# Four rows of the first pair read from stacked q and k, and the low-rank weights converted over more slots

## The chip, the cores and the metric

The kernel runs on one core of a Trainium2 chip. The metric is the device time of one execution in microseconds (us), as the median of three runs. The profile is one further execution, recorded by the hardware profiler. Engines are named as the trace names them: PE is TensorE's matmul, PEld its weight load, DVE is VectorE, ACT is ScalarE, POOL is GpSimd, and SP is SyncE, which only issues transfers. A trailing q (SPq, ACTq) is an engine's instruction queue.

## What is computed

An attention with a threshold feeds two token-mixing blocks. The part that the change touches is the attention and the low-rank mix behind it; the dense products behind them are named because their weights are converted meanwhile.

```python
scores = scale * (q @ k.T)                      # 4 batches, 8 heads, 576 rows, 64 wide
thresh = max(scores, axis=-1) - tau
attn = exp(where(scores >= thresh, scores, -1e9) - max)
attn = attn / (sum(attn) + 1e-9)
x = (attn @ v)                                  # heads side by side: 512 wide
u = x + (x.T @ U @ V).T                         # U: 576 x 32, V: 32 x 576
y = u + relu(u @ w_ch1) @ w_ch2                 # 512 x 2048 and 2048 x 512
out = (sigmoid(causal_conv(y, conv_w)) * (y @ w_val)) @ w_out
```

The weights U, V, w_ch1, w_ch2, w_val, conv_w and w_out come in as 64-bit floats and are converted on the chip.

## The kernel before

**Pairs and slots.** Two heads make a pair; there are 16 pairs. A pair has nine row blocks of 128: row 0 holds the last 64 rows of both heads, rows 1, 3, 5, 7 are 128-row blocks of the first head, rows 2, 4, 6, 8 of the second. The loop over `s` walks 144 slots, one row block in each: slot `s` is row `s % 9` of pair `s // 9`. Every engine gets its instructions in the order in which the loop writes them, so the order is set by hand. In slot `s`, VectorE scales the scores of its row and takes the maximum (`soft_max`, L467), masks the exponentials of the row before (`soft_mask`, L492) and, in the first pair only, adds the threshold (L482; in the others GpSimd does it). ScalarE takes the exponential (L481) and copies transposed blocks out of PSUM (L517 and others). TensorE computes the scores of the next row (`next_scores`), and transposes the exponentials of the row two slots back (L508, L525). The scores have two PSUM tiles, so row s+1 can be computed once L467 of slot s-1 is done. The product with v (`pv`, L551 and L562) for rows 0 to 4 of a pair comes in its last slot, for rows 5 to 8 four slots later; then the result is transposed back (`back`) and divided by the sums into `ring`.

**Precision.** q and k are split into a high and a low part (`hi_lo_qk`, L356 and L359, for a later pair's transposed q and k). A score is hi x hi + hi x lo + lo x hi + lo x lo. For pairs from the second on, `stacks` copies the parts by SyncE's transfers into a tile `st` for each head: its first 64 partitions hold high q, the other 64 low q; below stand high k twice and low k twice. With 128 partitions in use, two matmuls for each half of 288 columns do a row. The first pair doesn't wait for such transfers: `st` of the first pair has q's high and low parts in that head's 64 partitions and zeros in the others (L639), and a row takes four matmuls for each half (first head, L453), or four for each of three pieces (second head, L446, since its columns stand in another order). The tiles `st` come from a pool of four.

**Weights.** A converter is a generator of steps (`from_f64`: L101 on ScalarE, L103, L106, L110, L114, L122 or L124, L129 on VectorE or GpSimd). `work.tick()` moves each of at most two live converters on by one step. `wtick` says in which slots a tick comes: in each of the first 18 slots and in slots 3, 4 and 8 once more, then in six of every 18 (`CONVERT_AT`). U and V (`setup_UV`, in two parts, 512 and 224 wide) begin in slot 4, the four row blocks of the first quarter of w_ch1 (`chunk(0, 0)`, loads on L160) in slot 6, w_ch2's in slot 110.

**The mix.** `mix_t` (L601, x by U), `mix_tt` (a transpose), `mix_ut` and `mix_u` (by V, adding x) of pair p come 16, 18, 20 and 20 slots after its first. The first pair's are the first to need U and V.

Of the kernel before, what the change touches and what calls it, by code (L numbers as in the profile page):

```python
# [22 lines left out]
F32R = mybir.dt.float32r  # L23
# [13 lines left out]
def attention_moe_kernel(  # L37
# [15 lines left out]
    nc = tc.nc  # L53
    B, H, S, D = q.shape
# [11 lines left out]
    SM = 512  # L66
    TL = S - SM
# [9 lines left out]
    def f(ap):  # L77
        return ap.bitcast(F32)
# [165 lines left out]
    CONVERT_AT = (0, 2, 9, 12, 13, 17)  # L244
# [14 lines left out]
    def attention(dense_front, dense_mid, dense_top, dense_left, dense_back):  # L259
# [9 lines left out]
        st_p = front.enter_context(tc.tile_pool(name="st", bufs=4, side="right"))  # L269
# [16 lines left out]
        st8 = [dict() for _ in range(NP)]  # L286
# [114 lines left out]
        def stacks(p, hh):  # L401
# [13 lines left out]
            nc.sync.dma_start(out=s[64:128, 0, :], in_=qk[a:a + 64, 3, :])  # L415
            st8[p]["st", hh] = st

        def tails(p):
            qk = st8[p]["qk"]
            t = bd[p % 2]  # L420
            for hh in range(2):
                a = hh * D
                for c, sl in ((0, 0), (1, 3)):
                    o, i = t[a:a + 64, c, a:a + 64], f(qk[a:a + 64, sl, SM:S])
                    nc.gpsimd.tensor_scalar(out=o, in0=i, scalar1=1.0, scalar2=0.0, op0=ALU.mult, op1=ALU.add)


        def scores(p, i):
            d = st8[p]
            s = s_ps.tile([128, 2, 512], F32, tag="s", name="s")  # L430
            if i == 0:
                qk, t = d["qk"], bd[p % 2]
                ops = [(t[:, 0, :], qk[:, 1, :]), (t[:, 1, :], qk[:, 1, :]), (t[:, 0, :], qk[:, 2, :])]
            else:
                c, hh = divmod(i - 1, 2)
                c *= 128
                if p:
                    st = d["st", hh]
                    lhs = st[:, 0, c:c + 128]
                    ops = [(lhs, st[:, 1, :]), (lhs, st[:, 2, :])]  # L440
                else:
                    ops = [(d["st", hh][:, m, c:c + 128], d["qk"][:, n, :]) for m in (0, 1) for n in (1, 2)]
                    if hh:
                        for o, n, a in ((s[:, 0], TL, SM), (s[:, 0, TL:], HS - TL, 0), (s[:, 1], HS, HS - TL)):
                            for m, (lhs, rhs) in enumerate(ops):
                                nc.tensor.matmul(  # L446
                                    o[:, 0:n], lhs, rhs[:, a:a + n], start=(m == 0), stop=(m == len(ops) - 1)
                                )
                        d["s", i] = s
                        return  # L450
            for n in range(2):
                for m, (lhs, rhs) in enumerate(ops):
                    nc.tensor.matmul(  # L453
                        s[:, n, 0:HS], lhs, rhs[:, n * HS:(n + 1) * HS], start=(m == 0), stop=(m == len(ops) - 1)
                    )
            d["s", i] = s
# [32 lines left out]
        def soft_mask(p, i):  # L489
            d = st8[p]  # L490
            e = row(p, i)
            nc.vector.scalar_tensor_tensor(  # L492
                out=e, in0=d.pop(("ns", i)), scalar=d.pop(("th", i))[:, 0:1], in1=e, op0=ALU.is_le, op1=ALU.mult,
                accum_out=d["sum"][:, i:i + 1],
            )
            if i == 8:
                t = d["sum"]
                nc.vector.tensor_scalar(out=t, in0=t, scalar1=1e-9, scalar2=None, op0=ALU.add)
                nc.vector.reciprocal(out=d["r"], in_=t)
# [137 lines left out]
        for hh in range(2):  # L637
            t = st8[0]["st", hh] = st_p.tile([128, 3, S], F32R, tag="st", name="st")
# [4 lines left out]
        for m in range(2):  # L643
# [7 lines left out]
            out=rv[0][:, 0:8 * R].rearrange("p (t r) -> p t r", t=4),  # L651
            in_=moe_U[0:SM, :].rearrange("(t p) r -> p t r", p=128),
# [3 lines left out]
        def load_V(a, o, c, n):  # L656
            for g in range(4):
                nc.gpsimd.dma_start(out=a[g * R:(g + 1) * R, o:o + n], in_=moe_V[:, c:c + n])
# [3 lines left out]
            out=qscale, in0=tau_sb, scalar1=0.0, scalar2=-(float(D) ** -0.5), op0=ALU.is_ge, op1=ALU.mult  # L662
# [13 lines left out]
        for m in range(4):  # L676
            for _, fn in late[m].pop(-2, []):
                fn()
        load_V(rv[1], 0, 2 * (FC - nu), 2 * (nu + S - FC))


        def setup_UV(part):
# [17 lines left out]
        def put(s, what, *a):  # L700
            slots[s].append((what, a))

        for p in range(NP):
            s0 = 9 * p
            end = p == NP - 1
            for i in range(9):
                put(s0 + i + 2, trans_main, p, i)
                if i % 2 == 0:
                    put(s0 + i + 2, trans_tail, p, i)
            put(s0 + 8, pv, p, *(0, 1))  # L710
            v2 = s0 + (13 if end else 12)
            put(v2, pv, p, *(2,))
            put(v2 + 1, back, p)
            if p + 1 < NP:
                for what, at, *a in ((prep_T, (-3, 0), "q"), (prep_T, (1, 1), "k"), (prep_T, (2, 2), "tail"),
                    (stacks, (3, 5), 0), (tails, (4, 5)), (stacks, (5, 3), 1)):
                    put(s0 + at[not p], what, p + 1, *a)
            put(s0 + (15 if end else 16), mix_t, p)
            put(s0 + (17 if end else 18), mix_tt, p)
            put(s0 + (18 if end else 20), mix_ut, p)  # L720
            put(s0 + (18 if end else 20), mix_u, p)
        def next_scores(s):
            scores(*divmod(s + 1, 9))

# [2 lines left out]
        for s in range(NS):  # L727
            p, i = divmod(s, 9)
            slot[0] = s
            live = p < NP  # L730
            ev = slots[s]
            if s == 4:
                work.add(setup_UV(0))
                work.add(setup_UV(1))
            if s == 6: chunk(0, 0)
            if s == 110: chunk(0, 1)
            work.width = 2 if s < 9 * NP - 9 else 4
            def wtick(at):
                if at == 0 and (s < 18 or s % 18 in CONVERT_AT) or at == 1 and s in (3, 4, 8):
                    work.tick()  # L740
            wtick(-1)
            if live:
                soft_max(p, i)
            for m in (0, 1, 2, 3):
                for _, fn in sorted(late[m].pop(s, []), key=lambda x: x[0]):
                    fn()
                if m == 1 and live:
                    soft_exp(p, i)
                if m == 0 and 1 <= s <= 9 * NP:
                    soft_mask(*divmod(s - 1, 9))  # L750
                wtick(m)
            wtick(4)
            if s + 1 < 9 * NP:
                ev = [(next_scores, ())] + ev
            for what, a in sorted(ev, key=lambda x: 9 if x[0] in last else ORDER.get(x[0].__name__, 5)):
                what(*a) if what in last else what(s, *a)
            if i == 0 and p + 2 < NP:
                loads.append(load_qk(p + 2))
            if i == 4 and p + 1 < NP:
                loads.append(load_v(p + 1))  # L760
            load(2)
            if s == 9 * NP - 1:
                front.close()
                steps = next(dense_front)
                later(s + 1, 3, lambda: list(steps))
            if s == 9 * NP:
                ps_s.close()
            if s == 9 * NP + 1:
                mid.close()
                dense_mid()  # L770
            if s == 9 * NP + 5:
                top.close()
                dense_top()
                work.finish()
                chunk(1, 0)
            if s >= 9 * NP:
                next(dense_front, None)
                for _ in range(1 if lots else 1):
                    work.tick()
# [16 lines left out]
    def chunk(c, part):  # L796
        if c < NCH:
            src = w_ch2[c * FC:(c + 1) * FC, :] if part else w_ch1[:, 2 * c * FC:2 * (c + 1) * FC]
        else:
            src = w_out if part else w_val  # L800
        if 1 <= c < NCH and not part:
            loaded_rows = []
            for kk in range(KD):
                work.add(stage_rows(loaded_rows, kk, src[kk * 128:(kk + 1) * 128, :], c))
            work.add(combine(rows.setdefault((c, part), []), loaded_rows, c))
            return
        for kk in range(KD):
            work.add(weight_rows(rows.setdefault((c, part), []), (w2 if part else w1)[c % 2], kk, src[kk * 128:(kk + 1) * 128, :],
              (nc.vector if part else nc.vector) if c == 0 else nc.gpsimd,
              *(((0, 0, nc.gpsimd) if part else (0, 0, nc.gpsimd)) if c == 0 else ())))  # L810
# [490 lines left out]
```

## Time and profile before

| | |
|---|---|
| median of three runs | 802.89 us (802.13, 802.89, 803.55) |
| the profiled execution's own time | 802.15 us |
| its span, first to last instruction | 800.1 us |
| PE busy | 794.1 us (99%) |
| DVE busy | 684.2 us (86%) |
| ACT busy | 438.9 us (55%) |
| POOL busy | 196.9 us (25%) |
| granted TensorE clock over the span | 1.00 |

The attention's slots run from 9.56 us (first L467) to about 306 us; the rest of the span is dense products. Busy shares are averages over stages. A matmul's end is modelled, and neighbours overlap, so the interval between starts tells more than a duration does. A row of the chain says what held up the last instruction at that time, a row of the timeline what an engine did.

### The profile page before, as it was taken

How to read it: one execution, taken by the hardware profiler on the slowest of the kernel's cores; microseconds unless marked ns; L12 is line 12 of the kernel's file. 1: busy time of each engine (PE TensorE's matmuls, PEld its weight loads, DVE VectorE, ACT ScalarE, POOL GpSimd, SP SyncE). 2: the span in 40 equal slices, each digit the busy share in tenths (PEclk: the TensorE clock that was granted, in tenths of full speed). 3: DMA queues.
4: the chain of work that ended last, by engine and by line, in shares of the span. 5: the costliest groups of instructions: out<-in, count | busy, mean ns of one | idle time of the engine just before them, and what ended most of it. 6: DMA issues, size and time to landing. Idle time of an engine off the chain costs nothing.

```text
span 800.1 us, 15270 instructions
## 1 busy us (share of the span) xinstructions
PE 794.1 (99%) x5292; PEld 721.4 (90%) x5292; DVE 684.2 (86%) x1484; ACT 438.9 (55%) x943; POOL 196.9 (25%) x280
## 2 busy tenths in 40 slices
PE   9999999999999999999999999999999999999998
PEld 8788888888888888788899999999999999988887
DVE  7999999988888999579979799689999998988740
ACT  6888988888888888453423225123343343355421
POOL 4633533433333342030141004200342110000000
PEclk9999999999999999999999999999999999999999
DMA  7766776666667453556768658377477573001112
GB/s 166 185 149 149 171 171 152 145 142 137 149 160 167 105 132 134 168 181 252 279 224 309 219 198 302 111 271 288 165 274 261 188 246 119 1 1 52 54 53 79
DMA packets 97685, 134.20 MB, mean 168 GB/s; under 512 B 51285, under 2 KB 62309, under 8 KB 97610
## 3 DMA queue, kind: packets, MB, share of 16 engines
q1 hardware_dynamic: 96074, 132.24, 54.6%
q8 instruction: 42, 0.69, 0.3%
q0 software_dynamic: 336, 0.74, 0.3%
q10 hardware_dynamic: 1200, 0.26, 0.2%
q14 instruction: 33, 0.27, 0.1%
HBM read 85.43 MB, written 21.23 MB: 133 GB/s over the span
## 4 chain that ended last, share of the span: by engine, by line
PE 95%; DVE 3%; issue 1%; DMA 0%; SPq 0%; DVEq 0%
PE s L453 10%; PE c L1197 9%; PE a L1197 9%; PE a L1159 8%; PE c L1159 8%; PE xm L508 7%; PE o L562 7%; PE a L903 6%; PE v L903 6%; PE c L903 6%; PE p L1099 6%; PE xs L601 2%; PE o L551 2%; PE tm L380 2%; PE xs L562 1%; PE xs L525 1%
## 5 line engine op out<-in xcount | busy, mean ns | idle before, releaser
L467 DVE TENSOR_SCALAR_CACHE_REDUCE ns<-s,scalars 128x576 f32<-128x576 f32 x144 | 116.6, 810 | 18.1 <-PE s L453 17.5
L482 POOL TENSOR_TENSOR th<-nm,scalars 128x1 f32<-128x1 f32 x135 | 86.7, 642 | 161.1 <-DVE ns L467 158.2
L492 DVE SCALAR_TENSOR_TENSOR e<-ns,th,e 128x576 f32<-128x576 f32 x144 | 118.9, 826 | 0.0
L481 ACT ACTIVATE e<-ns,nm 128x576 f32<-128x576 f32 x144 | 112.2, 779 | 8.2 <-DVE ns L467 6.6
L453 PE MATMUL s<-st 128*128 128x288 f32 x480 | 94.2, 318 | 0.1
L517 ACT ACTIVATE pt<-xm 128x512 f32<-128x512 f32 x144 | 85.9, 597 | 4.5 <-PE xm L508 3.0
L508 PE MATMUL xm<-idn,e 128*128 128x128 f32 x576 | 86.8, 273 | 0.0
L1197 PE MATMUL a<-region,w 128*128 128x384 f32 x432 | 81.1, 335 | 0.2 <-DVE region L1130 0.2
L1197 PE MATMUL c<-region,w 128*128 128x384 f32 x432 | 80.7, 334 | 0.0
L453 PEld LDWEIGHTS s<-st 128*128 128x128 f32 x480 | 68.6, 191 | 12.3 <-issue 7.3
L1136 ACT ACTIVATE region<-c_sb 128x384 fp32r<-128x384 f32 x72 | 37.5, 524 | 73.4 <-DVE c_sb L1135 73.4
L1197 PEld LDWEIGHTS a<-region,w 128*128 128x128 f32 x432 | 75.3, 188 | 0.7 <-DVE region L1130 0.7
L1159 PE MATMUL a<-region,w_s 128*128 128x384 f32 x378 | 75.8, 334 | 0.0
L1159 PE MATMUL c<-region,w_s 128*128 128x384 f32 x378 | 75.6, 334 | 0.0
L1197 PEld LDWEIGHTS c<-region,w 128*128 128x128 f32 x432 | 75.5, 188 | 0.0
L508 PEld LDWEIGHTS xm<-idn,e 128*128 128x128 f32 x576 | 69.7, 143 | 0.7 <-issue 0.2
L174 POOL TENSOR_TENSOR w<-wf,w 128x512 fp32r<-128x512 f32 x20 | 29.0, 1451 | 162.3 <-ACT w L172 154.3
L1159 PEld LDWEIGHTS c<-region,w_s 128*128 128x128 f32 x378 | 66.4, 188 | 0.0
L1159 PEld LDWEIGHTS a<-region,w_s 128*128 128x128 f32 x378 | 66.3, 188 | 0.1
L562 PE MATMUL o<-pt,vt 128*64 128x256 f32 x512 | 61.5, 382 | 0.0
L562 PEld LDWEIGHTS o<-pt,vt 128*64 128x64 f32 x512 | 34.0, 137 | 19.2 <-issue 5.3
L1099 PE MATMUL p<-w,region 128*128 128x512 f32 (+1 forms) x228 | 49.8, 378 | 0.0
(166 smaller groups left out, 1514.6 us busy)
## 6 DMA issues: line engine op xcount, KB each, us to landing
region<-sp SPq DMA_DIRECT2D x126, 384.0 KB, 5.3
raw<-in_moe_w_ch_dram SPq DMA_DIRECT2D x32, 512.0 KB, 4.6
sp<-c_sb SPq DMA_DIRECT2D x24, 384.0 KB, 2.4
st<-qk SPq DMA_DIRECT2D x30, 256.0 KB, 3.4
st<-qk SPq DMA_DIRECT2D x45, 144.0 KB, 3.4
st<-qk SPq DMA_DIRECT2D x15, 432.0 KB, 4.0
out_dram<-c_sb SPq DMA_DIRECT2D x17, 256.0 KB, 2.0
st<-qk SPq DMA_DIRECT2D x15, 288.0 KB, 4.8
```

Of the source, the lines that this page charges most:

```text
L453: nc.tensor.matmul(s[:, n, 0:HS], lhs, rhs[:, n * HS:(n + 1) * HS], start=(m == 0), stop=(m == len(ops) - 1))
L467: nc.vector.tensor_scalar(out=ns.rearrange("p (a b) -> p a b", a=2), in0=s, scalar1=qscale[:, 0:1], scalar2=3.0e38, op0=ALU.mult, op1=ALU. ...
L481: nc.scalar.activation(out=row(p, i), in_=d["ns", i], func=ACTF.Exp, bias=nm[:, 0:1], scale=-1.0)
L482: (nc.gpsimd if p or 0 else nc.vector).tensor_tensor(out=th, in0=nm, in1=tau_eff, op=ALU.add)
L492: nc.vector.scalar_tensor_tensor(out=e, in0=d.pop(("ns", i)), scalar=d.pop(("th", i))[:, 0:1], in1=e, op0=ALU.is_le, op1=ALU.mult, accum_o ...
L508: nc.tensor.transpose(x[:, j * 128:(j + 1) * 128], e[:, c + j * 128:c + (j + 1) * 128], idn)
L517: later(s + 1, 0, lambda: nc.scalar.activation(out=dst, in_=x.rearrange("p (j c) -> p j c", j=4), func=ACTF.Copy), "x")
L562: nc.tensor.matmul(o, lhs, rhs, start=False, stop=stop)
L903: nc.tensor.matmul(ps[:, 0:m1], lhs, rhs, start=(m == 0), stop=(m == len(ops) - 1))
L1099: nc.tensor.matmul(ps, t[:, a, kk, sl], w[:, bb, kk, cols], start=(m == 0), stop=(m == 3 * KD - 1))
L1159: nc.tensor.matmul(ps, lhs, rhs, start=k == 0, stop=k == 5)
L1197: nc.tensor.matmul(ps, lhs, rhs, start=k == 0, stop=k == 3 * KD - 1)
```

## The change

Three things change. Rows 5 to 8 of the first pair are read from stacked tiles as those of the later pairs are: `first_stacks` makes them by four transfers on ScalarE's queue (first head) and six on SyncE's (second head), written just before slot 0. U and V are converted at one tick in each even slot up to slot 28, and slot 9, without the second ticks; from slot 30 to 62 only slots 36, 45 and 54 tick, and `chunk(0, 0)` begins at slot 24. The first pair's mix comes nine slots later, `mix_ut` and `mix_u` ten.

```diff
--- before.py
+++ after.py
@@ -415,6 +415,22 @@
             nc.sync.dma_start(out=s[64:128, 0, :], in_=qk[a:a + 64, 3, :])
             st8[p]["st", hh] = st
 
+        def first_stacks(hh):
+            qk, t = f(st8[0]["qk"]), f(st8[0]["st", hh])
+            a = slice(hh * D, (hh + 1) * D)
+            st = st_p.tile([128, 3, S], F32R, tag="st", name="st")
+            s = f(st)
+            eng = (nc.scalar, nc.sync)[hh]
+            for m in range(2):
+                o = slice(m * D, (m + 1) * D)
+                if hh:
+                    eng.dma_start(out=s[o, 1:3, TL:S], in_=qk[a, 1:3, 0:SM])
+                    eng.dma_start(out=s[o, 1:3, 0:TL], in_=qk[a, 1:3, SM:S])
+                else:
+                    eng.dma_start(out=s[o, 1:3, :], in_=qk[a, 1:3, :])
+                eng.dma_start(out=s[o, 0, 0:SM], in_=t[a, m, 0:SM])
+            st8[0]["first", hh] = st
+
         def tails(p):
             qk = st8[p]["qk"]
             t = bd[p % 2]
@@ -434,8 +450,8 @@
             else:
                 c, hh = divmod(i - 1, 2)
                 c *= 128
-                if p:
-                    st = d["st", hh]
+                if p or i >= (5, 6)[hh]:
+                    st = d["st" if p else "first", hh]
                     lhs = st[:, 0, c:c + 128]
                     ops = [(lhs, st[:, 1, :]), (lhs, st[:, 2, :])]
                 else:
@@ -677,6 +693,8 @@
             for _, fn in late[m].pop(-2, []):
                 fn()
         load_V(rv[1], 0, 2 * (FC - nu), 2 * (nu + S - FC))
+        for hh in range(2):
+            first_stacks(hh)
 
 
         def setup_UV(part):
@@ -715,10 +733,10 @@
                 for what, at, *a in ((prep_T, (-3, 0), "q"), (prep_T, (1, 1), "k"), (prep_T, (2, 2), "tail"),
                     (stacks, (3, 5), 0), (tails, (4, 5)), (stacks, (5, 3), 1)):
                     put(s0 + at[not p], what, p + 1, *a)
-            put(s0 + (15 if end else 16), mix_t, p)
-            put(s0 + (17 if end else 18), mix_tt, p)
-            put(s0 + (18 if end else 20), mix_ut, p)
-            put(s0 + (18 if end else 20), mix_u, p)
+            put(s0 + (15 if end else 16 if p else 25), mix_t, p)
+            put(s0 + (17 if end else 18 if p else 27), mix_tt, p)
+            put(s0 + (18 if end else 20 if p else 30), mix_ut, p)
+            put(s0 + (18 if end else 20 if p else 30), mix_u, p)
         def next_scores(s):
             scores(*divmod(s + 1, 9))
 
@@ -732,11 +750,11 @@
             if s == 4:
                 work.add(setup_UV(0))
                 work.add(setup_UV(1))
-            if s == 6: chunk(0, 0)
+            if s == 24: chunk(0, 0)
             if s == 110: chunk(0, 1)
             work.width = 2 if s < 9 * NP - 9 else 4
             def wtick(at):
-                if at == 0 and (s < 18 or s % 18 in CONVERT_AT) or at == 1 and s in (3, 4, 8):
+                if at == 0 and (s < 30 and s % 2 == 0 or s % 18 in (0, 9) or s > 62 and s % 18 in CONVERT_AT) or at == 1 and s in ():
                     work.tick()
             wtick(-1)
             if live:
```

## Rows read from the trace of the kernel before

**Rows 1.** The page: busy time, share of the span, instructions.

```profile
PE 794.1 (99%) x5292; PEld 721.4 (90%) x5292; DVE 684.2 (86%) x1484; ACT 438.9 (55%) x943; POOL 196.9 (25%) x280
```

**Rows 2.** Busy time by stretch, each engine's; last PE clock, DMA share, GB/s.

```profile
7.00:12.00 5.00, 5.00 (x42) 4.79 (x41) 4.40 (x14) 2.62 (x5) 1.21 (x3) 1.00 1.07 259
12.00:16.00 4.00, 4.00 (x37) 4.00 (x35) 4.00 (x13) 3.36 (x9) 0.00 (x0) 1.00 0.20 44
16.00:22.00 6.00, 6.00 (x53) 6.00 (x51) 6.00 (x19) 4.99 (x10) 4.28 (x5) 1.00 0.79 175
22.00:28.50 6.50, 5.91 (x58) 4.79 (x59) 6.50 (x20) 5.16 (x12) 2.54 (x4) 1.00 0.80 198
```

**Rows 3.** Chain of waits, 8 to 49 us: start, us, what.

```profile
12.62 1.05 PE s L453 x8
...
14.33 1.43 PE s L446 x12
...
16.68 0.73 DVE ns L467 x2
17.41 0.74 DVE e L492 x2
...
20.10 0.50 DVE wt L106
20.61 0.07 DVE th L482
...
22.15 0.64 DVE wf L110
...
24.56 0.34 DVE wt L114
...
25.27 0.61 DVE qk L359
...
25.93 0.70 PE o L551 x2
...
28.97 0.72 PE s L453 x4
...
30.13 0.53 PE s L453 x4
...
41.83 1.03 PE xs L601 x10
...
44.13 0.44 PE xm L508 x4
```

**Rows 4.** Timeline of VectorE, slots 4 to 10: start, us, instruction.

```profile
16.60 0.81 DVE L467 TENSOR_SCALAR_CACHE_REDUCE ns<-s,scalars 128x576 f32<-128x576 f32 x1
...
25.80 0.80 DVE L467 TENSOR_SCALAR_CACHE_REDUCE ns<-s,scalars 128x576 f32<-128x576 f32 x1
...
26.53 1.21 DVE L492 SCALAR_TENSOR_TENSOR e<-ns,th,e 128x576 f32<-128x576 f32 x1
...
29.85 0.63 DVE L129 TENSOR_TENSOR wf<-wf,wt 128x512 f32<-128x512 f32 x1
30.40 0.81 DVE L467 TENSOR_SCALAR_CACHE_REDUCE ns<-s,scalars 128x576 f32<-128x576 f32 x1
```

**Rows 5.** Timeline of all engines up to 24 us; in brackets idle time before.

```profile
10.42 0.78 ACT L481 ACTIVATE e<-ns,nm 128x576 f32<-128x576 f32 x1 [2.33 <-DVE ns L467]
...
15.35 0.51 SPq L411 DMA_DIRECT2D st<-qk  x1
...
23.18 1.54 SPq L415 DMA_DIRECT2D st<-qk  x1
```

**Rows 6.** Transfers issued 21.9 to 24 us: KB, us from issue to landing.

```profile
st<-qk SPq DMA_DIRECT2D x1, 144.0 KB, 5.3
```

**Rows 7.** Chain of waits, 60 to 130 us: VectorE's part's ends.

```profile
71.36 0.02 DVEq L359
...
79.09 0.81 PE s L453 x4
```

## Prediction

> **What bounds the kernel now.** I read the page first: TensorE is busy for 99% of the span [rows 1], so a shorter TensorE programme looks like time at once. A mean over stages says nothing of one stage, so I then read busy times by stretch around the first pair. There TensorE and VectorE are both full, from 12 to 22 us to the last hundredth, and the transfers leave gaps [rows 2]. The chain of waits decides between them. The reader is to see three stages in it [rows 3]. Up to about 16 us it is TensorE. From there to 25.9 us it is VectorE: row operations, and between them the conversion of U and V (L106, L110, L114). From 25.9 us it is TensorE, and almost only TensorE to the end. The timeline of VectorE gives the slots: the first operation of a slot's row (L467) starts at 16.60 us in slot 4, at 25.80 in slot 8 and at 30.40 in slot 10 [rows 4].
>
> So TensorE work taken out of slots 4 to 7 is worth nothing unless VectorE's work goes from there too, and the change does both. What I ask is when slot 10 can begin, and what the stretch behind it costs.
>
> **The rows read from stacks.** Row 5 or 7 has 8 matmuls of 288 columns, row 6 or 8 has 12 smaller ones; they hold the chain for 1.05 and 1.43 us. A stacked row has 4 and holds it for 0.53 [rows 3]. TensorE loses 2 x 0.52 + 2 x 0.90 = 2.84 us of work in slots 4 to 7. That is the cap on this part, and it comes out only as far as VectorE follows.
>
> **VectorE in slots 4 to 7.** The bare slot is 0.73 + 0.74 + 0.07 = 1.54 us (L467, L492, L482) [rows 3]. Four of them and the low part of the next q (0.61, L359) are 6.77. The stretch took 25.80 - 16.60 = 9.20 [rows 4]. The other 2.43 are conversion steps (0.50 + 0.64 + 0.34 for the 512-wide half; some 0.5 for the 224-wide half, estimated by its width); the 0.4 that is left I put down to GpSimd's conversion steps, which hold VectorE up. Counting ticks by the new rule (one each even slot, and slot 9), the first VectorE step of U falls in slot 8, where it was 5. The conversion steps leave the stretch. GpSimd's steps, and so the hold-up, may stay. Slot 8 then begins at 16.60 + 6.77 = 23.4, at most 23.8 us: 2.0 to 2.4 earlier. TensorE needs some 4.5 us for these four slots, so it doesn't bind.
>
> **When slot 10 can begin.** Three things must be there for row 10, which is pair 1's row 1.
>
> VectorE: slots 8 and 9 took 4.60 us, in which L492 was held for 0.40 (1.21 against 0.81) and the last step of U (L129) took 0.55, the time to the next start [rows 4]. Without these and the 0.2 of a small step, 3.45 are left; moved in are 0.50 + 0.64 and about 0.2, so 4.8. VectorE could begin slot 10 at 28.2 to 28.6.
>
> TensorE: from the end of slot 7's L359 the product with v and row 10's scores take 25.93 to 29.69 = 3.76 us [rows 3]. That gives 27.2 to 27.6 and doesn't bind.
>
> The transfers: row 10 reads pair 1's first stack, written by three transfers. The last was issued at 23.18 us, when SyncE came to it, and landed 5.3 us later [rows 5, 6], at 28.48. Before, this was hidden: TensorE came to row 10 only at 28.97 [rows 3], half a microsecond later. SyncE's issues ahead of it hang on the first slots and on their own number, not on slots 4 to 7, so the landing doesn't come earlier with VectorE. Row 10's scores can begin at 28.5 and take 0.6; slot 10 begins at about 29.15. Against 30.40 that is 1.25 us gained, where VectorE alone would give 1.8 to 2.2.
>
> **What the new transfers do to that landing.** The ten transfers of the change carry 2 x 288 + 2 x 128 KB for the first head and as much for the second, 1.66 MB in all. In 16 to 22 us the queue moved 175 GB/s at a share of 0.79 [rows 2], 220 at full share. At that rate they take all sixteen engines for 7.7 us; if the first head's long rows go at some 350, an estimate, for 6.2. They join a stretch that is full until 12 us (1.07). Idle were 0.80 x 4 = 3.2 us in 12 to 16, 1.3 in 16 to 22 and 1.3 in 22 to 28.5, together 5.8 [rows 2]. So between 0.4 and 1.9 us don't fit ahead of the landing. Against that, some of what ran at the end of that stretch was issued behind the stack and can wait. Bounds: no delay, and 1.9 us. I take 0.5.
>
> By the Trainium skill ("DMA: Bandwidth & Descriptors", section "Issuing engines are not separate DMA queues"), transfers issued from different engines run on the same sixteen engines and interleave, so half of them on ScalarE's queue saves issue time alone. By that rule the delay is the 0.5 just taken; if ScalarE's queue had bandwidth of its own it would be 0. No row before shows it, since ScalarE issues only the first q loads.
>
> **ScalarE's four issues.** They stand in its queue between its last copy and the first exponential, where it idles 2.33 us up to 10.42 [rows 5]. Behind them wait that exponential, then VectorE's L492 of row 0. An issue took from 0.51 us (the first stack transfer) to 1.54 (one behind a full queue) [rows 5]. Four take 2.0 to 6.2 us, so the exponential comes 0 to 3.9 late. I take 0.55 each, 2.2, no delay, since the first two find little of their own queue ahead; a delay up to 0.6 is hidden by the wait at slot 10. SyncE's six push the loads of v and of the next q by 3.6 us, into the gap before 15.35, where its next stack waits for data [rows 5].
>
> **From slot 10 to pair 1's product with v.** From L467 of slot 10 to the transposes ahead of that product (L508 at 44.13) it was 13.73 us, of which pair 0's token mix held TensorE 1.03 (L601) [rows 3, 4]. That goes to slot 25, where the chain is TensorE's; it is paid there again. So the stretch counts 12.70. VectorE, which is full here too, gets 0.34 and two small steps of about 0.3 and 0.2 and loses one of 0.3, and the GpSimd product of U that now falls into slot 14 may hold it up by 0 to 0.40. The stretch costs 12.7 to 13.1; I take 0.2 more than before. The rest of the mix (transpose, two products) moves to slots 27 and 30 at equal cost.
>
> **The first chunk.** By the ticks its VectorE steps go from slots 18 to 71 to slots 45 to 107, its row loads from about 30 us to slot 24 and later; from slot 110 on both programmes tick alike, so nothing is late for the dense part. Before, VectorE stood in the chain once between 46 and 310 us, from 71.36 to 79.09 [rows 7], where two rows' L114, L110 and L124 met in slots 30 and 31. After it, the same kinds meet in slots 66 and 67, the same places of a pair. I cost this at 0. Ends: 0.5 gained if the later meeting is covered, 0.5 lost if the doubled steps of slot 74 bind as well.
>
> **The sum.** +1.25 at slot 10, -0.5 for the transfers, -0.2 behind: 0.55, say 0.6 us gained. The profiled execution's own time is 802.15 (span 800.1 and 2.05 around it), so 801.55; the median of the three runs lies 0.74 higher, so 802.3. A gain below 0.2% (1.6 us) can't be told from no change here; the three runs themselves span 1.4.
>
> **Rivals.**
> *VectorE alone sets slot 10.* If the stack lands by 28 us, the gain is 1.95 - 0.2 = 1.75: 801.1. For it: the gap of 12 to 16 us, and the loads that wait behind. Against: the issue at 23.18 doesn't hang on what is shortened. Chance 0.24.
> *The transfers' backlog.* If the ten take 7.7 us and only the 4.5 idle up to 22 us help, pair 1's first stack is 3.2 late and lands at 31.7; slot 10 begins at 32.4, 2.0 later than before: with the 0.2, 805.1. It costs time from a landing of about 29.5 on and is measurable from 31.1. For it: the full share in 7 to 12. Against: the queue isn't idle-free later either, and a part of the bytes goes in long rows. Chance 0.14.
> *ScalarE's issues at 1.54 each.* The first exponential is 3.9 late; 28.4 + 3.9 = 32.3 for slot 10, 1.9 later than before: 805.0. Against: that row stood behind 720 KB. Chance 0.06.
> *The change brings nothing at slots 4 to 7*, because first stacks land past 17.4 us, where row 5 is wanted, and TensorE waits as long as it saves: 802.9. Chance 0.04.
> *The forecast*, 802.3, keeps 0.52; its own range is 801.4 to 803.3.
>
> Faster by over 0.2%: 0.17 of the first rival and 0.06 of the forecast (if the meeting in slot 30 vanishes as well), 0.23. Slower: 0.12 and 0.06, 0.18. Same: 0.59. The range goes from the first rival with that half microsecond (800.7) to short of the backlog's full price (804.4).
>
> **What would show it.** In the new profile: L467 of slot 8 at 23.4 to 23.8; rows 5 to 8 with four matmuls each; TensorE idle ahead of row 10's scores, released by the stack's transfer, and slot 10 at 29.2 to 29.7; pair 1's L508 ahead of the product with v at 42.0 to 42.6; two L601 groups side by side in slot 25; the chain TensorE's from there. Wrong would be the forecast if SyncE came to pair 1's first stack at another time than 22 to 23.5 us, if the first exponential began past 11 us, or if VectorE entered the chain in slots 63 to 76 for longer than it did before in slots 30 to 33.

## The result and the profile after

The changed kernel takes 808.80 us (median of six runs, 808.45 to 811.29) against 802.74 (six runs); the ratio is 1.008 with a 95% interval of 1.007 to 1.009. It is 6.1 us slower, where 0.6 us faster was forecast, and above the range's upper end of 804.4. The profiled execution took 808.85 us, with a span of 806.8.

Line numbers moved by 16: L467 is now L483, L492 is L508, L482 is L498, L481 is L497, L453 is L469, L508 is L524, L601 is L617. In `first_stacks` L430 and L431 are ScalarE's, L427, L428 and L431 SyncE's.

The page's busy times and the stretches of [rows 1, 2], with one stretch more:

```profile
PE 795.6 (99%) x5268; PEld 722.6 (90%) x5268; DVE 686.0 (85%) x1484; ACT 438.9 (54%) x943; POOL 196.4 (24%) x280
```
```profile
7.00:12.00 5.00, 4.82 (x41) 4.60 (x40) 4.26 (x11) 1.85 (x6) 1.23 (x3) 1.00 1.11 260
12.00:16.00 4.00, 4.00 (x34) 3.83 (x34) 3.47 (x10) 3.45 (x7) 0.00 (x0) 1.00 1.07 219
16.00:22.00 6.00, 3.96 (x24) 3.53 (x24) 5.83 (x19) 4.84 (x12) 3.28 (x5) 0.85 0.89 203
22.00:28.50 6.50, 6.50 (x61) 6.01 (x61) 6.09 (x18) 5.52 (x12) 0.96 (x1) 0.88 0.80 200
28.50:35.00 6.50, 3.18 (x24) 2.47 (x21) 3.15 (x11) 1.29 (x4) 0.80 (x2) 0.91 0.82 180
```

TensorE has 24 matmuls fewer and is yet busy for 1.5 us longer; the busy line doesn't say where the loss is. The stretches do. The gap of 12 to 16 us in the transfers is filled (share 1.07, was 0.20), and from 28.5 to 35 us TensorE and VectorE both stand for half of the time. What they wait for is in the chain of waits and in TensorE's timeline (last bracket: idle time before, and its releaser):

```profile
14.46 5.52 DMA st<-st
...
20.31 1.30 PE s L469 x4
...
26.77 0.12 SPq L407
...
26.93 0.59 SPq L408
...
27.57 5.36 DMA st<-qk
32.94 0.25 issue
33.18 0.77 PE s L469 x4
```
```profile
18.40 0.78 PE L469 MATMUL s<-st 128*128 128x288 f32 x4 [1.45 <-DMA st<-qk]
20.31 1.30 PE L469 MATMUL s<-st 128*128 128x288 f32 x4 [0.58 <-DMA st<-st]
...
33.18 0.77 PE L469 MATMUL s<-st 128*128 128x288 f32 x4 [3.32 <-DMA st<-qk]
```

Rows 5 and 6 wait 1.45 and 0.58 us for the new stacks; row 10 waits 3.32 us for pair 1's first stack. That one landed 5.36 us after its issue, as before (5.3, [rows 6]); what is late is the issue, 27.57 against 23.18 [rows 5]. SyncE's and ScalarE's timelines say why (the stack's first transfer is L407; below them that row before the change):

```profile
7.70 0.63 SPq L427 DMA_DIRECT2D st<-qk  x1
...
9.14 1.55 SPq L431 DMA_DIRECT2D st<-st  x1
10.74 0.67 SPq L427 DMA_DIRECT2D st<-qk  x1
13.77 0.59 SPq L428 DMA_DIRECT2D st<-qk  x1
14.46 0.55 SPq L431 DMA_DIRECT2D st<-st  x1
...
17.02 1.85 SPq L310 DMA_DIRECT2D qn<-in_q_dram  x2
...
19.61 0.57 SPq L411 DMA_DIRECT2D st<-qk  x1
...
26.38 0.51 SPq L407 DMA_DIRECT2D st<-qk  x1
...
27.57 1.51 SPq L415 DMA_DIRECT2D st<-qk  x1
```
```profile
7.84 0.53 ACTq L430 DMA_DIRECT2D st<-qk  x1
...
8.50 1.04 ACTq L431 DMA_DIRECT2D st<-st  x1
9.72 1.30 ACTq L430 DMA_DIRECT2D st<-qk  x1
11.11 0.56 ACTq L431 DMA_DIRECT2D st<-st  x1
11.72 0.78 ACT L497 ACTIVATE e<-ns,nm 128x576 f32<-128x576 f32 x1 [3.09 <-DVE th L498]
```
```profile
21.99 0.51 SPq L407 DMA_DIRECT2D st<-qk  x1
```

SyncE's six issues last from 7.70 to 15.01 us; between 11.4 and 13.77 it stands, and the view of waits (us in total, times, longest) names an earlier transfer:

```profile
SPq L428 <- DMA st<-qk: 2.3, 1, 2.3
```

The loads behind follow without a gap, and pair 1's second stack is begun at 19.61 where it was 15.35 [rows 5]. ScalarE's four issues took 3.8 us with the gaps between them, and the first exponential begins at 11.72 (10.42 before). VectorE's slots, as in [rows 4] (slots 4, 8 and 10):

```profile
17.90 0.81 DVE L483 TENSOR_SCALAR_CACHE_REDUCE ns<-s,scalars 128x576 f32<-128x576 f32 x1
...
25.93 0.81 DVE L483 TENSOR_SCALAR_CACHE_REDUCE ns<-s,scalars 128x576 f32<-128x576 f32 x1
...
33.99 0.82 DVE L483 TENSOR_SCALAR_CACHE_REDUCE ns<-s,scalars 128x576 f32<-128x576 f32 x1 [3.21 <-PE s L469]
```

From these starts the loss can be booked stretch by stretch. Each column is the time between two starts of that line, in us; slots 45 to 62 take 37.6 to 37.7 in every kernel, and the last slot begins at 306.17 before and at 313.02 after. Each row is one profiled execution; most took within about 1 us of their kernel's median, those of f3 and f4 1.6 us more.

| | start | slot 1 | slots 4-7 | 8-9 | slot 10 at | 10-17 | 18-44 | 63-80 | 81-142 |
|---|---|---|---|---|---|---|---|---|---|
| before | 9.56 | 2.15 | 9.20 | 4.60 | 30.40 | 14.66 | 56.89 | 37.66 | 128.89 |
| after | 10.10 | 2.91 | 8.03 | 8.06 | 33.99 | 16.59 | 57.32 | 38.21 | 129.24 |
| e1_stacks_only | 10.10 | 2.92 | 9.20 | 6.48 | 33.60 | 16.01 | 56.99 | 37.67 | 129.73 |
| e2_no_stacks | 9.55 | 2.14 | 7.89 | 4.86 | 29.34 | 16.33 | 57.01 | 38.20 | 128.94 |
| e3_unread | 9.93 | 2.98 | 7.83 | 8.77 | 34.40 | 16.11 | 57.28 | 38.18 | 128.93 |
| e4_unread_thin | 9.56 | 2.79 | 7.82 | 6.29 | 31.34 | 17.61 | 56.51 | 38.21 | 129.16 |
| e5_order | 10.10 | 2.88 | 7.37 | 4.74 | 29.98 | 16.36 | 56.54 | 38.23 | 128.88 |
| e6_clock | 9.71 | 4.45 | 7.36 | 8.40 | 34.80 | 16.32 | 56.61 | 38.18 | 128.91 |
| e7_mix_only | 10.10 | 2.15 | 9.20 | 4.60 | 30.94 | 14.52 | 58.23 | 37.66 | 128.90 |
| e8_chunk_only | 9.72 | 2.14 | 9.20 | 4.60 | 30.56 | 14.67 | 56.80 | 38.19 | 128.88 |
| e9_product | 9.59 | 3.98 | 7.36 | 4.74 | 30.57 | 16.58 | 57.52 | 38.44 | 129.15 |
| c1_later | 10.09 | 2.15 | 7.89 | 4.20 | 29.22 | 15.76 | 58.31 | 38.27 | 130.03 |
| c2_half | 10.18 | 4.28 | 7.21 | 4.27 | 30.84 | 15.76 | 58.34 | 38.27 | 130.05 |
| f2_no_uv | 9.62 | 2.15 | 7.89 | 5.72 | 30.27 | 14.87 | 57.07 | 37.66 | 128.88 |
| f3_change_no_uv | 9.61 | 3.30 | 6.78 | 4.18 | 28.77 | 15.19 | 60.44 | 38.23 | 128.91 |
| f4_early | 10.11 | 2.15 | 7.90 | 4.20 | 29.25 | 14.87 | 63.96 | 37.67 | 128.89 |

The start differs by half a microsecond between kernels that are alike up to there (before 9.56, e7 10.10), so those 0.54 are not the change's. The rest of the 6.85 us: slot 1 +0.76, slots 4 to 7 -1.17, slots 8 and 9 +3.46, slots 10 to 17 +1.93, 18 to 44 +0.43, 63 to 80 +0.55, 81 to 142 +0.35.

### The profile page after: what moved, and what is told of

Its sections match the earlier page's. It is cut to its first block, busy times and chain, and to the rows that moved or that the text cites. A ratio compares the mean times of both kernels' runs of the same rounds, so it can differ in the third digit from the quotient of the medians.

```text
span 806.8 us, 15244 instructions
## 1 busy us (share of the span) xinstructions
PE 795.6 (99%) x5268; PEld 722.6 (90%) x5268; DVE 686.0 (85%) x1484; ACT 438.9 (54%) x943; POOL 196.4 (24%) x280
## 4 chain that ended last, share of the span: by engine, by line
PE 93%; DVE 3%; DMA 1%; issue 1%; ACT 0%; ACTq 0%; SPq 0%; POOL 0%; DVEq 0%; POOLq 0%
PE s L469 10%; PE c L1215 9%; PE a L1215 9%; PE xm L524 8%; PE a L1177 8%; PE c L1177 7%; PE o L578 6%; PE a L921 6%; PE v L921 6%; PE c L921 6%; PE p L1117 6%; PE xs L617 2%; PE o L567 2%; PE tm L380 2%; PE xs L578 1%
## 5 line engine op out<-in xcount | busy, mean ns | idle before, releaser
L483 DVE TENSOR_SCALAR_CACHE_REDUCE ns<-s,scalars 128x576 f32<-128x576 f32 x144 | 116.8, 811 | 20.9 <-PE s L469 20.4
L498 POOL TENSOR_TENSOR th<-nm,scalars 128x1 f32<-128x1 f32 x135 | 86.7, 643 | 171.4 <-DVE ns L483 169.6
L508 DVE SCALAR_TENSOR_TENSOR e<-ns,th,e 128x576 f32<-128x576 f32 x144 | 119.4, 829 | 0.7 <-ACT e L497 0.7
L497 ACT ACTIVATE e<-ns,nm 128x576 f32<-128x576 f32 x144 | 112.1, 779 | 8.7 <-DVE ns L483 4.0
L469 PE MATMUL s<-st 128*128 128x288 f32 x496 | 98.7, 321 | 6.2 <-DMA st<-qk 4.8
L469 PEld LDWEIGHTS s<-st 128*128 128x128 f32 x496 | 72.1, 194 | 18.7 <-issue 9.9
L524 PE MATMUL xm<-idn,e 128*128 128x128 f32 x576 | 88.2, 277 | 0.0
L524 PEld LDWEIGHTS xm<-idn,e 128*128 128x128 f32 x576 | 71.0, 144 | 0.4 <-ACT e L497 0.2
```

The lines of the kernel that those rows point to most:

```text
L469: nc.tensor.matmul(s[:, n, 0:HS], lhs, rhs[:, n * HS:(n + 1) * HS], start=(m == 0), stop=(m == len(ops) - 1))
L483: nc.vector.tensor_scalar(out=ns.rearrange("p (a b) -> p a b", a=2), in0=s, scalar1=qscale[:, 0:1], scalar2=3.0e38, op0=ALU.mult, op1=ALU. ...
L497: nc.scalar.activation(out=row(p, i), in_=d["ns", i], func=ACTF.Exp, bias=nm[:, 0:1], scale=-1.0)
L498: (nc.gpsimd if p or 0 else nc.vector).tensor_tensor(out=th, in0=nm, in1=tau_eff, op=ALU.add)
L508: nc.vector.scalar_tensor_tensor(out=e, in0=d.pop(("ns", i)), scalar=d.pop(("th", i))[:, 0:1], in1=e, op0=ALU.is_le, op1=ALU.mult, accum_o ...
L524: nc.tensor.transpose(x[:, j * 128:(j + 1) * 128], e[:, c + j * 128:c + (j + 1) * 128], idn)
```

## The experiments

Times are medians; a ratio is to the kernel before, with its 95% interval.

**The parts alone.** e1_stacks_only is the change with the old ticks, mix and first chunk; e2_no_stacks is the kernel before with the new ticks, mix and chunk.

```diff
# e1: after, with
-if s == 24: chunk(0, 0)
+if s == 6: chunk(0, 0)
... (mix_t 16, mix_tt 18, mix_ut and mix_u 20 for all pairs; wtick as in the kernel before)
# e2: after without first_stacks, rows 5 to 8 read as before
```

> The changed kernel with the conversion ticks, the mix of pair 0 and the first chunk back in their old slots: only the ten transfers and rows 5 to 8 read from their tiles are left of the change. Transfer theory (the ten transfers make SyncE come some 4 us later to pair 1's first stack, so row 10 waits and TensorE's clock falls after the wait): that stack's first transfer is issued at 25 to 27 us, row 10 is released by it after 31, and the time is 805 to 808 us. Schedule theory (the moved conversions and the moved mix cost the time): 801 to 803.5 us.

> The kernel before with the new ticks, the mix of pair 0 nine slots later and the first chunk from slot 24, without the ten transfers and with rows 5 to 8 read as before. Transfer theory: pair 1's first stack is issued at 22 us as before, and the time is 802.5 to 804.5 us (the second mix in slot 25 costs 1.0, some of it is won back in slots 4 to 7). Schedule theory: 807 to 809 us.

e1 took 806.62 (1.0049, 1.0035 to 1.0063), e2 804.13 (1.0020, 1.0010 to 1.0029). The transfers lose most, but the other half loses too. In e2 SyncE comes to the stack as before, TensorE's row 10 waits for its landing, and slot 10 follows:

```profile
23.34 1.76 SPq L415 DMA_DIRECT2D st<-qk  x1
```
```profile
28.54 0.76 PE L453 MATMUL s<-st 128*128 128x288 f32 x4 [0.62 <-DMA st<-qk]
```
```profile
29.34 0.82 DVE L467 TENSOR_SCALAR_CACHE_REDUCE ns<-s,scalars 128x576 f32<-128x576 f32 x1
```

The prediction had 28.5 and 29.15 for the last two. The microsecond gained there is gone by slot 17 (16.33 against 14.66). e1 loses there too, though nothing was moved into these slots: behind the late stack they take 16.01, and TensorE was granted 0.55 and 0.60 of its clock in 34 to 36 and 36 to 38 us.

e7_mix_only is the kernel before with the first pair's mix moved as in the change; e8_chunk_only is the kernel before with the chunk begun at slot 24 and the new ticks from slot 18 on.

```diff
# e7
-put(s0 + (15 if end else 16), mix_t, p)
+put(s0 + (15 if end else 16 if p else 25), mix_t, p)
... (mix_tt 27, mix_ut and mix_u 30 for p = 0)
# e8
-if s == 6: chunk(0, 0)
+if s == 24: chunk(0, 0)
-if at == 0 and (s < 18 or s % 18 in CONVERT_AT) or at == 1 and s in (3, 4, 8):
+if at == 0 and (s < 18 or s < 30 and s % 2 == 0 or s % 18 in (0, 9) or s > 62 and s % 18 in CONVERT_AT) or at == 1 and s in (3, 4, 8):
```

> The kernel before with pair 0's mix nine slots later (ten for its last products) and nothing else. By the term of the sum, mix_t goes from a stretch where VectorE is as full as TensorE to one where TensorE alone binds: 0.7 to 1.1 us slower than before, 803.4 to 803.8 us. If the move is free, 802.6.

> The kernel before with the first chunk from slot 24 and the new ticks from slot 18 on; U and V at the old ticks, the mix in its old slots, no stacks. By the sum it is even: what two rows' steps cost together in slots 30 and 31 is lost in slots 66 to 74 in its place; 802.3 to 803.2 us. If the doubled steps of slots 63 to 74 cost more, 803.2 to 804; if they are covered there, 802.1.

e7 took 803.58 (1.0013, 1.0004 to 1.0022): slots 10 to 17 gave back 0.14 and slots 18 to 44 paid 1.34. e8 took 803.10 (1.0004, 0.9995 to 1.0013): its time can't be told from even. By its slots the chunk is not quite free: 63 to 80 take 0.53 more (0.5 to 0.8 in every other kernel with the new ticks), and 18 to 44 only 0.09 less.

**The transfers.** e3_unread is the whole change with rows 5 to 8 read the old way. e4_unread_thin does the same, and each of the ten transfers carries about a ninth of its bytes.

```diff
# e3 and e4
-if p or i >= (5, 6)[hh]:
-    st = d["st" if p else "first", hh]
+if p:
+    st = d["st", hh]
# e4 too
-eng.dma_start(out=s[o, 1:3, :], in_=qk[a, 1:3, :])
+eng.dma_start(out=s[o, 1:3, 0:TL], in_=qk[a, 1:3, 0:TL])
... (the others cut likewise)
```

> The changed kernel with its ten transfers, but rows 5 to 8 read the old way, so nothing reads the new tiles. Transfer theory: pair 1's first stack is still issued after 25 us and the time is 806 to 809 us. Reading theory (the short rows leave TensorE idle, and this and its clock cost the time, whatever the transfers do): 802.5 to 804.5 us, as without stacks.

> As the run with unread tiles, with the same ten transfers carrying a ninth to an eighth of the bytes each (64 columns of 512 or 576, and 8 of 64); the tiles are not complete and nothing reads them. If bytes set the delay: pair 1's first stack is issued at 22 to 23 us and the time is within 1 us of the run without stacks. If the number of issues and their waits for one another set it: issued after 25 us, time as with full unread transfers.

e3 took 809.70 (1.0085, 1.0071 to 1.0098), not told apart from the change, and a little above what was expected: whether rows 5 to 8 are read from the stacks hardly matters. It has the moved ticks and mix too, so what the transfers carry is what e3 has over e2, some 5.6 us. e4 took 807.26 (1.0056, 1.0044 to 1.0069), 2.4 us less than e3: of the 5.6 us, 3.1 are left with a ninth of the bytes. Pair 1's first stack is begun (L407) at 23.90 in e4, 26.38 in the change, 21.99 before: of the 4.4 us delay 1.9 come with the ten issues, even with little in them, and 2.5 with their bytes. Its row:

```profile
23.90 0.51 SPq L407 DMA_DIRECT2D st<-qk  x1
```

e5_order is the change with one number other: pair 1's first stack is issued in slot 3, ahead of its second.

```diff
-(stacks, (3, 5), 0), (tails, (4, 5)), (stacks, (5, 3), 1)):
+(stacks, (3, 3), 0), (tails, (4, 5)), (stacks, (5, 3), 1)):
```

> The changed kernel with one edit: SyncE issues both of pair 1's stacks in slot 3, the first head's ahead, so three of the nine transfers that row 10 doesn't need stand behind it, and so do the loads of slots 3 and 4. Transfer-order theory: the first head's stack is issued at 19.6 us in place of 26.4, lands by 28, row 10 no longer waits and TensorE's clock stays up after 30 us: 802.5 to 804.5 us. If the sixteen engines' load, not SyncE's order, sets the landing: it lands after 30 all the same, 806 to 809.

It took 804.67 (1.0026, 1.0015 to 1.0038): 4.1 us of the 6.1 are back. The stack's last transfer is issued at 20.68 and row 10 no longer waits; slot 10 begins at 29.98, though all ten transfers are still made.

```profile
20.68 1.84 SPq L415 DMA_DIRECT2D st<-qk  x1
```

So the late stack, with what follows from it, is shown to be the main loss, and its lateness a matter of SyncE's order.

e6_clock is the change with identity transposes on TensorE in slots 4 and 9, to hold its clock through the waits.

```diff
+if s in (4, 9):
+    warm(12 if s == 4 else 30)
```

> The changed kernel with idle transposes of the identity on TensorE, 12 in slot 4 ahead of row 5's scores and 30 in slot 9 ahead of row 10's, so that it works through the two waits. They cost nothing where it would wait (3.3 us at row 10). Clock theory: the granted clock stays at full in 19 to 24 and 33 to 37 us, slots 10 and 11 take 2.0 to 2.4 us less together with row 6's, and the time is 806 to 807.5 us. If the half clock costs nothing, because VectorE or the transfers bind there: 808.5 to 809.5.

In the change the granted clock fell to 0.50 (1.2 GHz) after these waits; rows of it, then of e6:

```profile
33.00:35.00 2.00, 1.82 (x10) 1.85 (x11) 1.01 (x3) 0.17 (x1) 0.11 (x1) 0.71 0.78 178
35.00:37.00 2.00, 2.00 (x11) 1.98 (x10) 2.00 (x7) 1.45 (x3) 0.59 (x1) 0.50 0.39 86
```
```profile
35.00:40.00 5.00, 4.97 (x39) 4.17 (x38) 5.00 (x14) 4.61 (x11) 1.50 (x3) 1.00 0.27 61
```

e6 kept 1.00 throughout and took 809.08 (1.0081, 1.0068 to 1.0093): no gain in time. In its profile slot 1 was 1.5 us longer than in the change's, so the stretch behind the wait is the better witness: slots 10 to 17 took 16.32 against 16.59. Slot by slot the clock does show. VectorE's rows in the change, then in e6:

```profile
38.20 0.69 DVE L359 TENSOR_TENSOR qk<-tm,qk 128x512 fp32r<-128x512 f32 x1 [0.53 <-ACT qk L356]
...
42.76 0.82 DVE L483 TENSOR_SCALAR_CACHE_REDUCE ns<-s,scalars 128x576 f32<-128x576 f32 x1 [0.34 <-PE s L469]
```
```profile
45.68 1.35 DVE L508 SCALAR_TENSOR_TENSOR e<-ns,th,e 128x576 f32<-128x576 f32 x1 [0.34 <-POOL th L498]
```

In the change VectorE waits in slots 11 and 13 for what TensorE delivers late (L356 copies its transposes), and slots 11 to 13 take 6.65 us, against 5.52 in e6, which has no such waits. In e6 slot 15 is held beside GpSimd's product and takes 2.45, against 1.57 in the change. The two nearly cancel. In slots 4 to 7 the change took 8.03 where e5, whose rows 5 and 6 wait 1.27 and 0.48 us at a clock of 1.00, took 7.37. So the clock is not the cause of the 6.1 us; by these profiles it costs at most 0.7 us in slots 4 to 7 and 0.3 net behind row 10, and no median shows it.

**Slots 10 to 17.** They are 1.7 us longer in e5 than before, with no late stack. The first theory was GpSimd's product of U (L122), which stands ahead of a threshold on that engine. e9_product is e5 with it on VectorE.

```diff
-w = yield from convert(raw_uv[part], 1, 1, nc.vector)
+w = yield from convert(raw_uv[part], 1, 0, nc.vector)
```

> The whole change with the order edit of e5_order, and besides U and V's second product with the weights' low part on VectorE (L124) in place of GpSimd (L122). Theory: the 1.7 us by which slots 10 to 17 are longer than before (16.4 against 14.66) come from that product: in slot 14 it stands on GpSimd ahead of that slot's threshold, and it holds VectorE up. Then slot 15 goes back from 2.5 to about 1.5 us, slots 10 to 17 take 15.7 to 16.0, VectorE pays some 0.3 to 0.5 for the product, and the time is 0.3 to 0.7 us below e5_order's 804.67: 804.0 to 804.4. Rival: the mere number of VectorE's conversion steps in slots 10 to 17 makes the difference; then slots 10 to 17 stay at 16.3 to 16.8 and the time is 804.7 to 805.2.

804.65 (1.0023, 1.0014 to 1.0033): nothing gained, and the eight slots still take 16.58. Slot 15 did fall from 2.45 to 1.47 us, but the product's 0.60 and 0.31 stand on VectorE instead. So it isn't GpSimd as such. VectorE's timeline of e5 between slots 10 and 17 shows what stands there beside the rows:

```profile
31.45 0.42 DVE L114 TENSOR_SCALAR wt<-wf 128x512 int32<-128x512 int32 x1
31.79 0.39 DVE L110 SCALAR_TENSOR_TENSOR wf<-raw,wt 128x224 int32<-128x224 int32 x1
...
35.64 0.28 DVE L114 TENSOR_SCALAR wt<-wf 128x224 int32<-128x224 int32 x1
...
40.90 1.36 DVE L508 SCALAR_TENSOR_TENSOR e<-ns,th,e 128x576 f32<-128x576 f32 x1 [0.34 <-POOL th L498]
...
43.66 0.68 DVE L129 TENSOR_TENSOR wf<-wf,wt 128x512 f32<-128x512 f32 x1
```

By the intervals to the next start these steps take 0.34, 0.30, 0.19 and 0.61, together 1.44; slot 15 waits 0.34 and is held 0.55 (1.36 in place of 0.81). Before, one step of 0.30 and one hold of 0.34 stood there. 2.33 less 0.64 is 1.69 of the 1.70. VectorE is busy for 16.02 of the 16.36.

To test it, U and V are left unconverted: one copy on ScalarE replaces every step on VectorE and the product on GpSimd. f2_no_uv does it to the kernel before, f3_change_no_uv to e5, and f4_early is f2 with e5's order edit.

```diff
-w = yield from convert(raw_uv[part], 1, 1, nc.vector)
+w = wst_p.tile([128, FC], F32, tag="wf", name="wf")[:, 0:n]
+nc.scalar.activation(out=w, in_=raw_uv[part][:, :, 1].bitcast(F32), func=ACTF.Abs)
...
```

> The kernel before with the same left out. Theory: slots 4 to 7 fall from 9.20 to 7.9, where TensorE binds as in e2_no_stacks; slot 10 begins at 29.1 to 29.4 (30.40 before), set by the landing of pair 1's first stack; slots 10 to 17 take 14.0 to 14.4 (14.66 before): the time is 800.8 to 801.5. It is the cap on what any other place for these steps can give, if all else stays. Rival: the steps cost nothing net in the old places, because something else comes last; then 802.4 to 803.

> e5_order (the whole change, pair 1's first stack issued first in slot 3), with U and V not converted: one copy on ScalarE takes the place of their steps on VectorE and of the product on GpSimd, so the mix multiplies by wrong weights. Theory: VectorE is full in slots 10 to 17 and pays for each step moved there; without them the eight slots take 14.5 to 15.0 us in place of 16.36, as in f1_no_uv (14.73) and f2_no_uv (14.87). Slots 8 and 9 lose 0.6 to 1.1 of their 4.74. The time is 801.8 to 802.8 (e5_order 804.67). Rival: the transfers or the order of TensorE's work lengthen the stretch; then it keeps 15.7 or more and the time is over 803.5.

> f2_no_uv (the kernel before, U and V not converted, the mix multiplies by wrong weights), with pair 1's two stacks both in slot 3, the first head's first. Theory: row 10 no longer waits for its stack (1.5 us in f2_no_uv), slot 10 begins at 28.3 to 29.0 and the time is 801.0 to 801.8: less than 2 us is all that the first ten slots can give, whatever is done with the conversion. Rival: what is gained at slot 10 is waited for later, by the second stack or by the mix; then 802.0 to 802.6, as in f2_no_uv.

f2 took 802.24 (0.9993, 0.9984 to 1.0002), f3 803.17 (1.0006, 0.9998 to 1.0015), f4 807.96 (1.0049, 1.0034 to 1.0065). A further run, f1_no_uv, is e7 with the same left out; it had been meant as f3, so what was expected of it doesn't apply. It took 802.76 (1.0003, 0.9994 to 1.0012), with slots 10 to 17 at 14.73.

In f3 the eight slots fall from 16.36 to 15.19, so the steps and the product are shown to cost 1.2 of the 1.7; they don't reach the 14.7 of f1 and f2, and the remaining half microsecond is open: VectorE waits there 0.58 us for scores and 0.17 and 0.22 for ScalarE, and no run shows what made them late. The time missed its expectation by 0.4 us. The chain of f3's profiled execution, 1.6 us above its median, shows a wait further on:

```profile
42.69 0.84 SPq L413
...
43.58 0.62 SPq L414
...
44.25 4.20 DMA st<-qk
...
48.69 0.86 PE s L469 x4
```

Slot 18 begins at 43.96, earlier than in any other kernel, and then row 20 waits for pair 2's stack: SyncE issues it in one row of transfers and comes to its last only 0.54 us earlier than in e5, 44.25 against 44.79 (slots 18 to 44 at 60.44). f4 misses likewise (slots 18 to 44 at 63.96, in the slowest of its executions): by its chain SyncE came to the next loads only when a load of v, issued behind two 512 KB weight loads, had landed, and a row then stood 4.13 us for the q so delayed.

```profile
39.55 8.95 DMA vt<-in_v_dram
```

And f2 says that the whole conversion of U and V, in its old place, costs some 0.5 us net (1.3 at the interval's end): without it row 10 waits 1.49 us for its stack.

**Looking for a better version.** c1_later drops the first pair's stacks, converts U and V in slots 14 to 25, and has e5's order; c1b_product has U's product on VectorE as well; c2_half adds to c1 the first head's four transfers on ScalarE's queue, with rows 5 and 7 alone read from them.

```diff
# c1, against the kernel before (mix moved as in e7, stacks as in e5)
-if s == 4:
+if s == 14:
     work.add(setup_UV(0))
...
-if s == 6: chunk(0, 0)
+if s == 24: chunk(0, 0)
-if at == 0 and (s < 18 or s % 18 in CONVERT_AT) or at == 1 and s in (3, 4, 8):
+if at == 0 and (14 <= s < 26 or s > 26 and s % 18 in CONVERT_AT):
# c2, against c1
+first_stacks(0)
-if p:
-    st = d["st", hh]
+if p or i >= (5, 9)[hh]:
+    st = d["st" if p else "first", hh]
```

> Without the ten transfers and the stacked rows of the first pair. U and V are converted with a tick in each of slots 14 to 25, the mix of the first pair stands as in the change, the first chunk begins at slot 24 and ticks by the old table after slot 26, and pair 1's two stacks are issued in slot 3, the first head's first. Theory: what the change earns is the conversion's absence from slots 4 to 8; without the transfers' price, and with the stack issued earlier, slot 10 begins at 28.3 to 28.8 (30.40 before), slots 10 to 17 without U's later steps take 14.7 to 15.5, the mix's term costs 0.9: 801.5 to 802.5, that is the same as before or a little faster. Rival: conversion steps cost as much in slots 14 to 25 as in 4 to 8, since VectorE is full there too; then 803 to 804.

> c1_later with the second product on VectorE in place of GpSimd. If GpSimd's product holds up thresholds in slots 14 to 25, this is 0.3 to 0.7 us faster than c1_later; if VectorE is what is full there, 0.3 to 0.7 us slower.

> c1_later, and besides the first head's four transfers alone on ScalarE's queue, with rows 5 and 7 alone read from the stack (1.04 us less for TensorE). Theory: ScalarE's four issues make the first exponential 0.5 to 0.9 us late, which is paid in slot 1; SyncE's queue, with six issues fewer than in the change, comes to the later pair's stack within 1 us of c1_later; TensorE's saving shows only where TensorE binds, in slots 4 to 7 without conversion: so 0.3 us faster to 0.6 slower than c1_later. Rival: the delay of SyncE comes from the bytes alone, whichever queue issues them; then L407 of pair 1's first stack comes over 2 us later than in c1_later, row 10 waits, and the time is 1.5 to 2.5 us longer than c1_later's.

c1 took 805.11 (1.0031, 1.0020 to 1.0043), c1b 806.06 (1.0041, 1.0029 to 1.0054), c2 806.67 (1.0048, 1.0035 to 1.0060). c1b is 0.95 slower than c1: as in e9, taking the product off GpSimd gains nothing. c1 is worse than even its rival had it: slot 10 begins at 29.22, but the steps are paid in slots 10 to 17 (+1.10) and, with the mix, in 18 to 44 (+1.42), and 0.61 and 1.14 are lost in the last two columns. The first of these is near e8's 0.53; the second I put down to the chunk's old ticks from a later start, without a run that shows it. In c2 four issues on ScalarE, with its waits between them, put the first exponential at 13.17 and slot 1 takes 4.28, 2.13 more than in c1, against 0.68 saved in slots 4 to 7. The 1.56 us over c1 and the 2.2 us by which SyncE comes later to L407 are the rival's numbers, but not by its mechanism: row 10 doesn't wait for its stack, and SyncE's wait ahead of L407 is for VectorE's L359, late with slot 1. No version beat the kernel before.

## Why the prediction was wrong, step by step

**What failed: the new transfers' delay of the landing, taken as 0.5 us, was 4.5.** The stack landed at 32.94, not 28.98; slot 10 began at 33.99, not 29.65. The failing sentence is "SyncE's six push the loads of v and of the next q by 3.6 us, into the gap before 15.35, where its next stack waits for data". Six issues took 7.3 us, 4.6 of them issuing and 2.3 waiting for an earlier transfer, and the loads behind them 4.5; the gap was overrun by 4.3, and since SyncE works in order, all of it reached pair 1's first stack. The bytes had been counted against idle transfer time; the queue's time at the issuing engine had been counted at its cheapest. The rival "the transfers' backlog" had the right place and nearly the right landing (31.7) with a chance of 0.14; its mechanism, bytes that don't fit, accounts for 2.5 of the 4.4 at most (e4), and e5 shows that order mends it with all bytes in place. No run shows the 350 GB/s from which its lower bound of 0.4 us came: while the ten ran, in 7 to 12 and 12 to 16 us, the queue moved 260 and 219 GB/s. Two of the conditions named for failure came true: SyncE at 26.38 and the first exponential past 11 us.

**ScalarE's four issues: forecast 2.2 us and no delay, measured 3.8 and 0.76** in slot 1 (up to 5.4 and 2.3 in e6, where 1.9 of the 5.4 are issues and the rest waits between them). In the change they cost 0.53, 1.04, 1.30 and 0.56, inside the bounds of [rows 5], above the value taken. The Trainium skill ("DMA: Bandwidth & Descriptors", "Issuing engines are not separate DMA queues") says that a second issuing engine saves issue time only. Here the time so saved on SyncE was charged to ScalarE, which had the exponential behind it.

**The stretch behind slot 10: forecast 0.8 less there and 1.03 more in slot 25, together +0.2; measured +1.93 in slots 10 to 17 (1.7 in e2 and e5) and +0.43 in 18 to 44.** Two terms failed. The 1.03 us of the mix were taken out of the stretch as if TensorE set it; VectorE is full there, e7 gave back 0.14 and paid 1.34 later. And the steps moved in were under-counted: the last step of U (0.61, L129) was credited to slots 8 and 9, where it was gone, and not charged in slot 16, where it came to stand. GpSimd's product cost VectorE 0.34 + 0.55 in slot 15 of e5, above the bound of 0.40; in the change that slot lost 0.1, and VectorE lost 0.53 and 0.34 waiting for TensorE's late results in its place.

**What held.** VectorE's floor for slots 4 to 7, 6.77 us: f3 took 6.78; the change itself took 8.03, where rows 5 and 6 waited for their stacks and TensorE was then granted about half its clock (e5, with similar waits and the full clock, 7.37). The rival of late first stacks, given 0.04, was met in part, but slots 4 to 7 still came out 1.17 shorter. That these rows bring nothing unless VectorE is relieved: e1 kept 9.20. That the stack's landing sets slot 10, at 29.15 with SyncE undisturbed: e2 has 29.34. That VectorE's place in the chain doesn't grow: from 153.18 to 160.87 in the change, 7.7 us, as long as before from 71.36 to 79.09 [rows 7]. The chunk's cost of 0 came out at its lower end instead, 0.53 lost in slots 63 to 80 with 0.09 won back (e8). So the forecast's gain would not have come with those transfers free either: e2, without them, is 1.5 us slower than before.

## What to carry to other kernels

Count a new transfer on the queue of the engine that issues it, at the issue times seen behind a full queue and with its waits, and follow that queue in order to the next transfer that someone waits for; here, with a ninth of the bytes, that transfer was still begun 1.9 us late. When steps are spread over later slots of an engine that is full there too, list each step in its new slot before crediting its old one: a step that moves within a full stretch is not a gain. Where three limits lie within 2 us of each other, as VectorE, the stack's landing and the next pair's transfers do here, lifting one yields little: leaving U's and V's conversion out altogether was worth about 0.5 us.

## What was not expected of the hardware

SyncE stood 2.3 us ahead of an issue (L428) whose source and target no earlier new transfer writes, until an earlier transfer had landed; the trace shows the wait and not its reason. An issue took about 0.5 to 0.7 us on either engine with little ahead of it, up to 1.55 in the change's full stretch, and 2.3 in f3 and f4. A 256 KB load of v took 8.95 us in f4, issued behind two 512 KB loads, where the median over the changed kernel's sixteen is 4.2. After waits of 1.45 and 0.58 us for stacks TensorE was granted 0.54 and 0.60 in 20 to 22 and 22 to 24 us, and after 3.32 us 0.71 and 0.50 in 33 to 35 and 35 to 37; after one of 1.49 us in f2 it kept 1.00. What the half clock cost behind row 10 was partly hidden: GpSimd's product of U began 1.13 us ahead of slot 15 in the change and 0.33 in e6, and only in e6 VectorE was held beside it.
